# Loading the first x block as four tiles in turn on two DMA queues, with one warm-up matmul fewer

## The chip, the cores and the metric

The kernel runs on one core of a Trainium2 chip. The metric is the device time of one execution in microseconds, lower is better. The profile shows a span that is 1.2 to 1.3 us shorter than the device time of the same execution. The granted TensorE clock shown for whole runs is 1.0, except 0.994 in two runs (295.44 us in experiment 5, 295.73 us in experiment 8) and 0.999 in one of e11_split_evac. That number does not show the first microseconds, in which the clock is at half speed; these are read from the spacing of the matmuls and, where a trace has them, from its clock records.

"Landing" below means the moment at which the last of the 16 DMA engines reported its share of a transfer done, read from the completion records of the trace. The Trainium skill, "DMA: Bandwidth & Descriptors", section "Why a DMA increments its semaphore by 16 and not by 1", says that only the full 16 means that all data has landed.

## The reference, cut to what matters

```python
x = A_x                                              # [1, 2048, 640] bf16
g = sigmoid((x * gate_w).sum(-1, keepdims=True))
a = linear_attention(x, wqkv, w_phi) @ wo            # 32 heads of 20, phi = two softmaxes per head
b = (gelu(x @ w_gate) * (x @ w_up)) @ w_down         # F = 1728
out = g * a + (1 - g) * b
```

The change touches only the loading of the first 512 rows of x, for the v, k and q projections.

## The kernel before

Five engines run in parallel. Matmuls need x with its columns on partitions ("xT"). Tiles 0 to 3 (the first block) are loaded plainly, transposed on TensorE (PE) and copied out by VectorE (DVE) and ScalarE (ACT). Tiles 4 to 15 and the weights wk and wq are transposed by the DMA on the way in. Each DMA queue is served by one engine's sequencer, in order: "sp" and "act".

```python
def loads(self):
    x4 = self.x[0:self.BT, :].rearrange("(p j) n -> p j n", j=self.TB)    # 4 tiles, j = tile
    def xload(q, j):                                     # two tiles, 320 KB, one DMA
        sc.dma(q, lambda e: e.dma_start(self.xtok[:, j:j + 2, :], x4[:, j:j + 2, :]),
               writes=[("xtok", j), ("xtok", j + 1)])
    ...
    xload("sp", 0)
    xload("act", 2)
    sc.dma("act", ... w_phi ...)                         # 640 packets of 40 bytes
    for kt in range(KD):
        sc.dma("sp", ... w3[:, kt, 0:D] ...)             # "wv" blocks 0 to 4, 160 KB each
    sc.dma("act", ... gz ...)
    xturn(4, 2)                                          # transposed load, x tiles 4 and 5 (sp)
    wload(self.wkT, D, "wkT")                            # transposed load of wk (sp)
    xturn(6, 2)                                          # x tiles 6 and 7 (sp)
    wload(self.wqT, 0, "wqT")                            # transposed load of wq (sp)
    ...                                                  # further loads, all on sp

def attention_state(self):
    ...
    warm(7)                                              # matmuls on zeros
    xt(0, 6, "d"); xt(1, 7, "a"); xt(2, 2, "d"); xt(3, 3, "a")   # PE transposes and their copies
    for t in range(4): vs(t, 0)                          # V matmuls with wv block 0; then blocks 1 to 4
    ...
    self.v_early(4, 6); self.v_early(5, 0)
    f(0, "k", (2, 3), "d"); f(1, "k", (4, 5), "a")       # folds of wk; the letter: who copies, d = DVE
    self.v_early(6, 6)                                   # first use of x tile 6
    f(2, "k", (2, 3), "d"); f(3, "k", (4, 5), "a"); f(4, "k", (0, 1), "d")
    self.v_early(7, 6); self.k_early(0, 2)
    f(0, "q", (4, 5), "d"); f(1, "q", (6, 7), "d")       # first use of wqT
    self.k_early(1, 0)
    f(2, "q", (4, 5), "d"); f(3, "q", (6, 7), "d")
    self.k_early(2, 2)
    f(4, "q", (4, 5), "d")
    self.k_norm(0)                                       # DVE, 3.6 us for each tile from here on
    ...
```

A fold multiplies a block of wk or wq by w_phi on PE, so that the projection and the feature map become one product; its result is copied out by DVE or ACT. k_norm sums the exponentials of one k tile by head and divides by the sums.

The softmax here doesn't subtract the row's maximum and nothing guards it: scores larger than these inputs give would overflow.

## Time and profile before

| | before |
|---|---|
| device time, first three runs | 291.62, 291.98, 292.02 us |
| span, PE busy | 290.6 us, 282.1 us |
| x load on SP / on ACT landed | 4.79 / 4.55 us |
| first wv block landed | 5.45 us |
| x tiles 6 and 7 landed, wqT landed | 15.19 us, 20.29 us |
| DVE's first k_norm | 25.66 us |

From the page of the kernel before (first line, and the first line of its busy table: engine, busy us, share, instructions):

```profile
span 290.6 us, 6966 instructions
PE 282.1 (97%) x2990; PEld 179.2 (62%) x3007; DVE 167.5 (58%) x337; ACT 105.2 (36%) x199; POOL 27.6 (10%) x52
```

The PE is busy nearly throughout, so what remains is in single waits. The timeline of PE in the first 17 us (start us, length us, engine, line, operation, tiles, and in brackets the idle time before it):

```profile
1.25 3.17 PE L538 MATMUL ps<-zero 128*128 128x512 bf16 x7 [1.25 <-DVE zero L534]
4.83 1.29 PE L290 MATMUL ps<-ident,xtok 128*128 128x128 bf16 x20 [0.41 <-DMA xtok<-in_A_x_dram]
5.96 4.72 PE L363 MATMUL ps<-w,xT 128*128 128x480 bf16 x32
...
15.23 1.53 PE L351 MATMUL ps<-w,xT 128*128 128x512 bf16 x10
```

The seven warm-ups start 427 ns apart, the 20 transposes only 56 ns apart: 512 columns in 427 ns is about half the rate of 128 columns in 56 ns, so the full clock came in this trace just when the transposes began. The waits of PE in the first 52 us (who waited for whom: us in total, times, longest):

```profile
PE ps L538 <- DVE zero L534: 1.3, 1, 1.3
PE ps L449 <- DVE Ek L433: 1.2, 1, 1.2
PE ps L290 <- DMA xtok<-in_A_x_dram: 0.4, 1, 0.4
PE ps L351 <- ACT Eq L516: 0.3, 1, 0.3
```

The second line: at 50.9 us PE waits for the k_norm chain of DVE. The chain of waits, up to x tile 6 (start us, length us, what):

```profile
3.74 2.28 SPq L224
...
6.07 4.20 SPq L220
...
10.32 4.87 DMA xT<-in_A_x_dram
15.19 0.04 issue
```

Here the chain goes back through SP's issues of transposed loads (2.28 us for x tiles 4 and 5, 4.20 us for wk), not through PE. DVE, in its timeline, starts k_norm right behind the copy of the last fold of wq:

```profile
24.92 0.82 DVE L344 CAST wq<-ps 128x640 bf16<-128x640 f32 x1 [0.43 <-PE ps L331]
25.66 1.48 DVE L424 TENSOR_REDUCE Dk<-Ek 128x64 f32<-128x1280 bf16 x1
```

### The profile page before, as it was taken

To read this page: it belongs to the slowest core of one execution; us is meant where nothing else is said; L and a number is where in the kernel's file an instruction comes from. 1 tells how busy PE (TensorE), PEld (TensorE's weight loads), DVE (VectorE), ACT (ScalarE), POOL (GpSimd) and SP (SyncE) were. 2 spreads that over 40 slices of the span, in tenths; PEclk is the share of its full clock that TensorE was granted. 3 is DMA by queue.
4 is the path that set the end of the run, shared out by engine and by line. 5 is a ranking of instruction groups with operands and counts; after the bars stand their busy time and mean duration, and the time that the engine had idled before them with its cause. 6 is when DMAs were issued, how large, how long until landed. Compare 5 with 4: busy or idle time off the path is not lost.

```text
span 290.6 us, 6966 instructions
## 1 busy us (share of the span) xinstructions
PE 282.1 (97%) x2990; PEld 179.2 (62%) x3007; DVE 167.5 (58%) x337; ACT 105.2 (36%) x199; POOL 27.6 (10%) x52
## 2 busy tenths in 40 slices
PE   7999998999999999999999999999999999999996
PEld 3666788699954444444477644447764444777786
DVE  2248999999876742677767533235753323575001
ACT  3367887576673223222202232320223232022021
POOL 7000000000000000011131300001130000113000
PEclk9999999999999999999999999999999999999999
DMA  7999995000002000011114220000322000042211
GB/s 226 198 177 250 367 366 168 0 2 2 2 0 45 2 0 0 3 24 23 25 25 44 74 68 0 0 3 2 52 66 68 0 0 2 2 43 74 68 48 49
DMA packets 36937, 18.66 MB, mean 64 GB/s; under 512 B 28970, under 2 KB 36394, under 8 KB 36906
## 3 DMA queue, kind: packets, MB, share of 16 engines
q1 hardware_dynamic: 36096, 17.86, 25.9%
q8 instruction: 23, 0.38, 0.6%
q10 hardware_dynamic: 810, 0.35, 0.5%
q14 instruction: 8, 0.07, 0.1%
HBM read 9.04 MB, written 2.62 MB: 40 GB/s over the span
## 4 chain that ended last, share of the span: by engine, by line
PE 82%; DVE 8%; SPq 3%; issue 3%; DMA 2%; ACT 2%; ACTq 0%
PE ps L620 36%; PE ps L710 27%; PE ps L351 13%; DVE Dk L424 2%; PE ps L653 2%; DVE Ek L433 2%; DMA xT<-in_A_x_dram 2%; PE ps L630 1%; SPq L220 1%; DVE KV L504 1%; PE ps L449 1%; DVE Dk L428 1%; ACT Ek L413 1%; PE ps L331 1%; SPq L224 1%
## 5 line engine op out<-in xcount | busy, mean ns | idle before, releaser
L625 DVE TENSOR_TENSOR hT<-ps,gl 128x512 bf16<-128x512 f32 x52 | 35.8, 691 | 57.4 <-PE ps L620 56.6
L710 PE MATMUL ps<-wd_sb,hT 64*128 64x320 bf16 (+2 forms) x918 | 66.3, 288 | 0.0
L620 PE MATMUL ps<-xT,wu_sb 128*128 128x512 bf16 x256 | 63.8, 379 | 1.2 <-DVE hT L625 1.0
L620 PE MATMUL ps<-xT,wg_sb 128*128 128x512 bf16 x250 | 62.9, 379 | 1.3 <-issue 1.0
L623 ACT ACTIVATE gl<-ps 128x512 bf16<-128x512 f32 x52 | 31.0, 598 | 72.8 <-PE ps L620 66.3
L710 PEld LDWEIGHTS ps<-wd_sb,hT 64*128 64x128 bf16 x918 | 42.8, 94 | 15.4 <-ACT gl L623 0.8
L682 POOL TENSOR_TENSOR Og<-O,O 128x640 bf16<-128x640 bf16 x16 | 22.3, 1396 | 239.8 <-DVE O L680 239.8
L620 PEld LDWEIGHTS ps<-xT,wu_sb 128*128 128x128 bf16 x260 | 25.4, 98 | 32.0 <-DVE hT L625 1.5
L620 PEld LDWEIGHTS ps<-xT,wg_sb 128*128 128x128 bf16 x260 | 24.8, 98 | 30.1 <-issue 0.9
L723 ACT ACTIVATE outsb<-ps,Gm 128x320 bf16<-128x320 f32 (+2 forms) x31 | 14.6, 516 | 75.3 <-PE ps L710 75.3
L351 PE MATMUL ps<-w,xT 128*64 128x512 bf16 (+6 forms) x398 | 41.4, 325 | 0.2
L351 PEld LDWEIGHTS ps<-w,xT 128*64 128x64 bf16 (+1 forms) x400 | 33.4, 107 | 7.3 <-DMA xT<-in_A_x_dram 0.2
L710 PE MATMUL ps<-wo_sb,goT 64*128 64x320 bf16 (+2 forms) x340 | 27.3, 288 | 0.0
L351 PE MATMUL ps<-xT,wq 128*64 128x512 bf16 (+1 forms) x184 | 25.8, 380 | 0.4 <-ACT Eq L516 0.3
L433 DVE TENSOR_TENSOR Ek<-Ek,Dk 128x640 bf16<-128x640 bf16 x32 | 25.0, 822 | 0.6
L680 DVE TENSOR_TENSOR O<-ps,RH 128x640 bf16<-128x640 f32 x32 | 24.8, 817 | 0.0
L424 DVE TENSOR_REDUCE Dk<-Ek 128x64 f32<-128x1280 bf16 x16 | 23.7, 1481 | 1.5 <-ACT gcol L416 1.5
L516 ACT ACTIVATE Eq<-ps 128x512 bf16<-128x512 f32 x40 | 21.7, 605 | 2.6 <-PE ps L351 2.3
L413 ACT ACTIVATE Ek<-ps 128x640 bf16<-128x640 f32 x32 | 20.8, 704 | 3.5 <-PE ps L351 3.5
L710 PEld LDWEIGHTS ps<-wo_sb,goT 64*128 64x128 bf16 x340 | 16.2, 94 | 5.6
L351 PEld LDWEIGHTS ps<-xT,wq 128*64 128x64 bf16 (+1 forms) x185 | 14.5, 108 | 4.1 <-ACT Eq L516 0.8
L669 DVE RECIPROCAL RH<-ps 128x32 f32<-128x32 f32 x16 | 5.7, 358 | 17.3 <-PE ps L653 17.3
(65 smaller groups left out, 145.6 us busy)
## 6 DMA issues: line engine op xcount, KB each, us to landing
out_dram<-outsb SPq DMA_DIRECT2D x7, 320.0 KB, 2.5
wd_sb<-in_B_w_down_dram SPq DMA_DIRECT2D x1, 2080.0 KB, 13.9
wg_sb<-in_B_w_gate_dram SPq DMA_DIRECT2D x1, 1120.0 KB, 6.0
wu_sb<-in_B_w_up_dram SPq DMA_DIRECT2D x1, 1120.0 KB, 8.5
wg_sb<-in_B_w_gate_dram SPq DMA_DIRECT2D x1, 960.0 KB, 9.6
wu_sb<-in_B_w_up_dram SPq DMA_DIRECT2D x1, 960.0 KB, 10.2
w<-in_A_wqkv_dram SPq DMA_DIRECT2D x5, 160.0 KB, 4.2
wo_sb<-in_A_wo_dram SPq DMA_DIRECT2D x1, 800.0 KB, 9.6
```

Of the source, the lines that this page charges most:

```text
L351: self.sc.op("pe", lambda e: e.matmul(self.ps[a:z, bank * 512 + c0:bank * 512 + c0 + n], lhs[:, a:z], rhs, start=first, stop=fin), reads=r ...
L413: self.sc.op("act", lambda e, s=s, scale=scale: e.activation(self.Ek[:, se, s, :], self.ps[:, o:o + self.D], AF.Exp, scale=scale), reads=[ ...
L424: sc.op("dve", lambda e: e.tensor_reduce(self.Dk[:, se, 0, :].rearrange("p (s h) -> p s h", h=H), self.Ek[:, se, :, :].rearrange("p s (h d ...
L433: sc.op("dve", lambda e, v=v, r=r: e.tensor_tensor(v, v, r, ALU.mult), reads=[("Rk", se)], writes=[("Ek", se, s)])
L516: sc.op("act", lambda e, s=s, scale=scale: e.activation(self.Eq[:, s, i, b * self.BT:(b + 1) * self.BT], self.bank(bank), AF.Exp, scale=sc ...
L620: sc.op("pe", lambda e, kt=kt, w=w, bk=bk: e.matmul(self.bank(bk), w[:, kt, c * P:(c + 1) * P], xs(kt), start=(kt == 0), stop=(kt == self. ...
L623: sc.op("act", lambda e: e.activation(self.gl[:, slot, :], self.bank(banks[0]), AF.Gelu_apprx_tanh), reads=[("ps", banks[0])], writes=[("g ...
L625: sc.op("dve", lambda e: e.tensor_tensor(hT[:, c, :], self.bank(banks[1]), self.gl[:, slot, :], ALU.mult), reads=[("ps", banks[1]), ("gl", ...
L680: dve(lambda e, o=o, f=f, s=s: e.tensor_tensor(o, V[s][:, :, :, 0:DH], f, ALU.mult), rb + [key(6 + s)], [("O", s, sl)], guard=old)
L682: sc.op("pool", lambda e: e.tensor_tensor(self.Og[:, sl, :], self.O1[:, sl, :], self.O2[:, sl, :], ALU.add), reads=[("O", 0, sl), ("O", 1, ...
L710: sc.op("pe", lambda e: e.matmul(self.bank(bk, w), lhs, rhs, start=opens and x == 0, stop=end and not opens, skip_group_check=True), reads ...
L723: sc.op("act", lambda e: e.activation(dst, self.bank(bk, w), AF.Copy, scale=g), reads=rd, writes=wr)
```

## The change

The intent: tiles 0 and 1 land first, so the transposes start earlier, and one warm-up matmul gives them room. Each queue now issues two x loads of 160 KB in place of one of 320 KB. One packet carries 1280 bytes where it carried 2560.

```diff
         def xload(q, j):
-            sc.dma(q, lambda e: e.dma_start(self.xtok[:, j:j + 2, :], x4[:, j:j + 2, :]),
-                   writes=[("xtok", j), ("xtok", j + 1)])
+            sc.dma(q, lambda e: e.dma_start(self.xtok[:, j, :], x4[:, j, :]), writes=[("xtok", j)])
...
-        xload("sp", 0)
-        xload("act", 2)
+        for j in range(4):
+            xload(("sp", "act")[j % 2], j)
...
-        warm(7)
+        warm(6)
```

## The prediction

> **What bounds the kernel.** The page shows the PE busy 282.1 of 290.6 us: the whole is TensorE-bound. The change touches only the first 25 us. From the timeline and the DMA landings:
> - Seven warm-up matmuls run from 1.25 to about 4.3 us, 427 ns apart (half clock). The two 320 KB x loads (2560 B packets, 102 ns each) are issued at 0.80 on SP and ACT and land at 4.79 and 4.55. The PE waits 0.41 us for them (waits view); the 20 transposes start at 4.83, 56 ns apart (full clock).
> - The V matmuls start at 5.96 (first wv block landed 5.45). They wait twice (0.13 and 0.05 us) for ACT's xT copies of 0.70 us, then run without a gap to 11.8.
> - At 15.23 the PE waits about 0.22 us for the transposed load of x tiles 6 and 7, landed 15.19. The transposed wq load lands at 20.29, its first user runs at 20.34: almost no slack.
> - From 25.66 to 51 DVE runs k_norm without a pause, started by the last q fold; the PE waits 1.35 us for that chain at 50.9.
> - The chain of waits goes back from 15.19 not through the PE but through SP's issues.
>
> **What the change does.** Each queue issues two 160 KB x loads in place of one of 320 KB.
> - At 55 ns per 1280 B packet (as the wv blocks show) I estimate tiles 0 and 1 landed at 3.9 to 4.1, tiles 2 and 3 at about 4.9. The transposes begin at about 4.0 instead of 4.83. ACT's first copy moves up by about 0.5 us, so the fourth tile's V matmul starts at about 6.5 instead of 6.95, and V ends about 0.4 us earlier.
> - One more SP issue (412 ns and a gap, about 0.47 us) stands before the wv blocks and all transposed loads. The wv blocks hardly move, since the DMA engines are full from 2.9 to 7 us. The transposed loads move later by between 0 (if full engines hold up their issue: equal ones took SP 2.28 and 1.41 us) and 0.47 us.
> - The warm-up matmul saves nothing itself: left in, it would hold up tile 0's transposes by up to 0.4 us.
>
> **What reaches the end.** The 0.4 us won in V is lost at 15.2 us, where the PE meets the load of tiles 6 and 7, no earlier than before. The end moves with that landing: 0 to +0.5 us, my middle +0.2.
>
> Predicted: 292.2 us, range 291.6 to 292.9; faster by over 2%: 0.01, within 2%: 0.98, slower by over 2%: 0.01.
>
> **What would show it.** Right: transposes begin near 4.0, the last V matmul ends near 11.4; the wait before the v projection of tile 6 grows from 0.2 to 0.6 us or more; tiles 6 and 7 land at 15.2 to 15.7; the DVE chain starts at 25.7 to 26.1. Wrong: that landing at 15.0 or earlier and DVE's chain earlier, a gain.
>
> **What could make it wrong.** The clock. The Trainium skill, "TensorE: Matmul & The Clock Gate", Part 1, says that about 3.4 us of sustained matmuls release the full clock, by a free-running window. The trace agrees in size: matmuls from 1.25, full clock from 4.85. Part 4 says that transposes don't count as busy in the same way, which no trace here tests. With six warm-ups the PE is busy only to about 3.8; if the release slips a window (to about 8.3), V runs at half clock meanwhile, and I estimate +1 to +1.5 us at the end: one chance in ten. The other: transposed loads that land earlier because the split x load speeds the engines up.

## The result, and the profile after

| | before | after |
|---|---|---|
| device time, median (lowest to highest) | 292.0 (291.62 to 292.67), 4 runs | 292.56 (292.22 to 292.89), 4 runs |
| x tiles landed (0, 1, 2, 3) | 4.79, 4.79, 4.55, 4.55 | 4.08, 3.87, 4.85, 4.61 |
| first wv block landed | 5.45 | 6.23 |
| x tiles 6 and 7 landed | 15.19 | 15.79 |
| DVE's first k_norm | 25.66 | 26.26 |
| span | 290.6 | 291.2 |

The ratio was 1.0017, with a 95% interval of 0.9995 to 1.0038: the same. Ratios here are the mean time of one kernel's fast runs over that of the other's of the same rounds, so not quite the ratio of the medians. From the page of the kernel after:

```profile
span 291.2 us, 6985 instructions
PE 284.0 (98%) x3006; PEld 180.0 (62%) x3006; DVE 167.3 (57%) x337; ACT 105.2 (36%) x199; POOL 27.6 (9%) x52
```

PE shows more busy time and more instructions because the trace of before lacks some matmul records, not because of the change. The timeline of PE after:

```profile
1.25 2.74 PE L537 MATMUL ps<-zero 128*128 128x512 bf16 x6 [1.25 <-DVE zero L533]
4.13 1.99 PE L289 MATMUL ps<-ident,xtok 128*128 128x128 bf16 x20
6.37 4.53 PE L362 MATMUL ps<-w,xT 128*128 128x480 bf16 x32 [0.25 <-DVE xT L297]
...
15.84 1.36 PE L350 MATMUL ps<-w,xT 128*128 128x512 bf16 x7 [0.46 <-DMA xT<-in_A_x_dram]
```

The transposes start 0.70 us earlier but take 1.99 us instead of 1.29, because the first 14 of them run 107 ns apart, at half clock; the full clock came at 5.64 us. The V matmuls (third line) start 0.41 us later than before. The profile names a DVE copy of xT as what they waited for, but the first V matmul reads only tile 0, whose copy was done at 5.37. What fits is the first wv block, landed at 6.23: in four traces with split loads where it landed after the transposes, the first V matmul starts 0.14 us behind it (6.23 and 6.37 here; 6.65 and 6.79, 6.19 and 6.33, 6.45 and 6.59 in later runs). The waits (three other lines left out) and the chain after:

```profile
PE ps L448 <- DVE Ek L432: 1.2, 1, 1.2
PE ps L350 <- DMA xT<-in_A_x_dram: 0.5, 1, 0.5
```

```profile
4.24 2.25 SPq L223
...
6.54 3.54 SPq L219
...
10.12 5.67 DMA xT<-in_A_x_dram
15.79 0.05 issue
```

The wait for the x tiles (L350) is new. SP began its transposed loads 0.50 us later than before (4.24 against 3.74), and tiles 6 and 7 landed 0.60 us later. From there all of DVE's work lies 0.60 us later:

```profile
25.52 0.82 DVE L343 CAST wq<-ps 128x640 bf16<-128x640 f32 x1 [0.44 <-PE ps L330]
26.26 1.48 DVE L423 TENSOR_REDUCE Dk<-Ek 128x64 f32<-128x1280 bf16 x1
```

So these two traces tell a neat story: one more issue on SP, a later landing, 0.6 us at the end. The experiments show that only part of it holds.

### The profile page after: what moved, and what is told of

Read it like the earlier page. It is cut to its first block, busy times and chain, and to the rows that moved or that the text cites. A ratio compares the mean times of both kernels' runs of the same rounds, so it can differ in the third digit from the quotient of the medians.

```text
span 291.2 us, 6985 instructions
## 1 busy us (share of the span) xinstructions
PE 284.0 (98%) x3006; PEld 180.0 (62%) x3006; DVE 167.3 (57%) x337; ACT 105.2 (36%) x199; POOL 27.6 (9%) x52
## 4 chain that ended last, share of the span: by engine, by line
PE 83%; DVE 8%; SPq 3%; issue 2%; DMA 2%; ACT 1%; ACTq 0%
PE ps L619 36%; PE ps L709 27%; PE ps L350 13%; DVE Dk L423 2%; PE ps L652 2%; DMA xT<-in_A_x_dram 2%; DVE Ek L432 2%; PE ps L629 1%; PE ps L448 1%; DVE KV L503 1%; SPq L219 1%; DVE Dk L427 1%; PE ps L330 1%; SPq L232 1%; SPq L223 1%
## 5 line engine op out<-in xcount | busy, mean ns | idle before, releaser
L619 PE MATMUL ps<-xT,wu_sb 128*128 128x512 bf16 x260 | 64.6, 379 | 1.0 <-DVE hT L624 1.0
L619 PE MATMUL ps<-xT,wg_sb 128*128 128x512 bf16 x260 | 64.7, 379 | 0.0
L350 PE MATMUL ps<-w,xT 128*64 128x512 bf16 (+6 forms) x400 | 41.9, 325 | 0.5 <-DMA xT<-in_A_x_dram 0.5
L350 PEld LDWEIGHTS ps<-w,xT 128*64 128x64 bf16 (+1 forms) x400 | 33.4, 107 | 7.7 <-DMA xT<-in_A_x_dram 0.6
L350 PE MATMUL ps<-xT,wq 128*64 128x512 bf16 (+1 forms) x185 | 26.1, 380 | 0.3 <-ACT Eq L515 0.3
L350 PEld LDWEIGHTS ps<-xT,wq 128*64 128x64 bf16 (+1 forms) x185 | 14.6, 109 | 4.0 <-ACT Eq L515 0.8
```

The lines of the kernel that those rows point to most:

```text
L350: self.sc.op("pe", lambda e: e.matmul(self.ps[a:z, bank * 512 + c0:bank * 512 + c0 + n], lhs[:, a:z], rhs, start=first, stop=fin), reads=r ...
L619: sc.op("pe", lambda e, kt=kt, w=w, bk=bk: e.matmul(self.bank(bk), w[:, kt, c * P:(c + 1) * P], xs(kt), start=(kt == 0), stop=(kt == self. ...
```

## The experiments

**The measure used for all of them.** In the traces with unaltered copies (12 of 14, from 290.64 to 294.50 us), the end of the span is DVE's first k_norm plus 264.95 to 265.00 us. And in all 14 that start is, within 0.01 us, the latest of three sums:

- V gate: the start of the 40th (last) V matmul plus 13.83 us
- x gate: the landing of x tiles 6 and 7 plus 10.47 us
- wq gate: the landing of wqT plus 5.36 us

The three constants were read off single traces, and the others agree with them; they were on record before the traces from e6_pad3 on existed. In the two runs with moved copies 1.26 us, read off these two, is to be taken off each sum. The table has the latest gate in bold; "full clock" is the time at which the matmul spacing changes or the trace's clock record begins, a range where neither tells it closer. The experiments from e6 on ran on other chips than those before them (7 for e1 to e4, 0 for e6 to e9, 8 from e10 on), so times are compared with those of before in the same round, while traces are compared across rounds. By the 2% rule every verdict below is "same"; "slower" means here only that the interval leaves out no change.

| trace | full clock | first wv block | 40th V | V gate | x gate | wq gate | first k_norm | span |
|---|---|---|---|---|---|---|---|---|
| before | 4.85 | 5.45 | 11.60 | 25.43 | **25.66** | 25.65 | 25.66 | 290.64 |
| e13_before (before again) | 6.9 to 7.2 | 5.35 | 12.51 | **26.34** | 25.64 | 25.16 | 26.34 | 291.32 |
| after | 5.64 | 6.23 | 11.80 | 25.63 | **26.26** | 26.01 | 26.26 | 291.24 |
| e1_repeat (after again) | 6.0 to 6.8 | 6.65 | 12.22 | **26.05** | 25.81 | 25.28 | 26.05 | 291.05 |
| e2_split_warm7 | 5.91 | 5.68 | 11.74 | 25.57 | 25.80 | **26.29** | 26.29 | 291.28 |
| e3_whole_warm6 | 6.7 to 7.0 | 5.22 | 12.31 | **26.14** | 24.59 | 24.78 | 26.14 | 291.12 |
| e4_split_act3 | 4.98 | 4.59 | 12.15 | **25.98** | 25.40 | 24.93 | 25.98 | 290.95 |
| e6_pad3 | 6.80 | 5.88 | 12.38 | 26.21 | **27.09** | 25.53 | 27.09 | 292.06 |
| e7_whole_relief | 6.30 | 5.44 | 12.11 | 25.94 | 25.65 | **26.57** | 26.58 | 291.54 |
| e8_split_relief | 4.69 | 6.19 | 12.08 | 25.91 | **26.23** | 26.07 | 26.22 | 291.18 |
| e9_split_relief_w0 | 4.56, lost 7.97, back 11.38 | 5.85 | 15.72 | **29.55** | 27.56 | 26.91 | 29.55 | 294.50 |
| e10_whole_evac | 6.68 | 5.24 | 12.34 | **24.91** | 23.58 | 23.46 | 24.91 | 289.98 |
| e11_split_evac | 5.33 | 6.45 | 12.03 | 24.60 | 25.03 | **25.21** | 25.22 | 290.46 |
| e12_pairs | by 5.5 | 6.12 | 12.26 | 26.09 | **26.25** | 25.60 | 26.25 | 291.24 |

**1. The changed kernel again (e1_repeat).** No edit.

> The changed kernel once more, unaltered, for a second trace and more times. Theory S (the end moves with the transposed load of x tiles 6 and 7, and one more issue on SP delays that landing): landing again at 15.5 to 15.8 us, DVE's first k_norm at 26.0 to 26.3, time 0.4 to 0.7 us over the kernel before. Rival P (the first changed trace was unlucky: one 1280 B packet took 993 ns, and the last of 16 engines' share of the first wv block landed 0.75 us behind the others): no such packet here, first wv block lands at about 5.5 instead of 6.23, V starts by 5.6, and the end is within 0.2 us of before.

Median 292.05 us in 6 runs, before 292.18 in 11 runs (291.35 to 292.62); ratio 1.0002 (0.9985 to 1.0020). The repeat shows no loss at all. DVE's start, 26.05, fell where theory S put it, but for another reason than S has: tiles 6 and 7 landed at 15.34 and were not waited for; the V gate was last. Rival P falls too: the first wv block landed even later (6.65), with 15 of 16 engines done at 6.23. So a fixed cost of 0.4 to 0.7 us over before, which S expected, did not show; the interval (about -0.4 to +0.6 us) leaves room for its lower half.

**2. Split load, seven warm-ups (e2_split_warm7).**

```diff
-        warm(6)
+        warm(7)
```

> The changed kernel with the seventh warm-up matmul put back. Theory S: the warm-up plays no part in the end, so time within 0.2 us of the changed kernel, landing of tiles 6 and 7 again 15.5 to 15.8; the first transpose starts about 0.15 us later than 4.13. Rival C (six warm-ups release the full clock too late: it came at 5.64 us against 4.85 before, 14 transposes ran at half clock): full clock at 4.7 to 5.0, transposes done by about 5.6 instead of 6.1, and the end 0.3 us or more earlier than the changed kernel.

Median 292.08, ratio 1.0000 (0.9983 to 1.0017). The time does not notice the seventh warm-up. The full clock came at 5.91, later than in the trace with six (5.64), so rival C falls. Tiles 6 and 7 landed at 15.33, and the wq gate was last this time.

**3. Whole loads, six warm-ups (e3_whole_warm6).**

```diff
-        warm(7)
+        warm(6)
```

> The kernel before with six warm-up matmuls instead of seven, nothing else. Theory S: SP's issues are untouched, so tiles 6 and 7 land at about 15.2 and the end is within 0.15 us of before, even if the first transposes run at half clock. Rival C: the full clock comes late (5.5 us or later), V ends later, and the end is 0.3 us or more later.

Median 292.08, ratio 1.0001 (0.9983 to 1.0018). All 20 transposes ran at half clock, and the V gate was the last. This looked like C's prediction until experiment 12 showed the same with seven warm-ups. The time is that of before.

**4. Tile 0 on SP, tiles 1 to 3 on ACT (e4_split_act3).**

```diff
-            xload(("sp", "act")[j % 2], j)
+            xload(("sp", "act", "act", "act")[j], j)
```

The ACT queue also got six lanes, so that it never waits for one.

> The split load with tile 0 on SP and tiles 1, 2, 3 on the ACT queue (with six lanes there), so that SP issues as many transfers as before. Theory S: SP's transposed loads are issued at the times of before, tiles 6 and 7 land at 15.0 to 15.3, and the end is within 0.2 us of before (0.4 to 0.6 us faster than the changed kernel). Rival D (the smaller 1280 B packets cost the DMA engines time, whoever issues them): landing stays at 15.6 or later and the end 0.4 us or more above before.

Median 292.37, ratio 1.0014 (0.9998 to 1.0030): no clear difference. The landing of tiles 6 and 7 (14.93) came back to where it was, as theory S says, and still nothing was won: tiles 2 and 3 landed at 5.71 and 6.22, the last transpose started at 6.50, and the V gate was the latest. Opening one gate brought up the next.

**5. Three tiny loads more on SP (e6_pad3).** (No run bears the name e5. The line that allocates the tile pad is left out.)

```diff
         xload("act", 2)
+        for k in range(3):
+            sc.dma("sp", lambda e: e.dma_start(self.pad[:, k, :], self.x[k * P:(k + 1) * P, 0:16]), writes=[("pad", k)])
```

> The kernel before with three tiny loads (128 rows of 32 bytes, into a tile nobody reads) put on the SP queue between the x load and the first wv block: three more SP issues of about 0.47 us, almost no bytes. Theory G (the start of DVE's k_norm chain is the latest of three gates, and the end is that start plus 264.98 us: the 40th V matmul plus 13.83 us, the landing of x tiles 6 and 7 plus 10.47, the landing of wqT plus 5.36; one SP issue ahead delays the landings by up to 0.47 each): landing of tiles 6 and 7 1.0 to 1.5 us later than the 15.19 of before, DVE start 26.6 to 27.2, time 0.9 to 1.5 us over before. Rival A (the engines are so full that SP's issue order in time does not matter): landing within 0.4 us of before and time within 0.3 us.

Median 293.33, ratio 1.0063 (1.0041 to 1.0086): clearly slower. Chain of waits of this run (L231 are the tiny loads, two further ones left out):

```profile
1.27 0.43 SPq L231
...
5.17 2.20 SPq L225
...
11.41 5.21 DMA xT<-in_A_x_dram
16.62 0.05 issue
```

SP began its transposed loads at 5.17 instead of 3.74, and tiles 6 and 7 landed at 16.62 instead of 15.19: 1.43 us in both, 0.48 for each issue. So a later issue on SP does pass to the landing, with almost no bytes moved. That it passed to the hundredth is chance: with SP's transposed loads begun at 3.74 or 3.75, tiles 6 and 7 landed as early as 14.12 (experiment 3) and 14.37 (experiment 9). The mean loss of 1.84 us (0.0063 of 292) is more than theory G's 0.9 to 1.5, but one run of 295.44 us raises it, which shows a granted clock of 0.994; the medians lie 1.33 apart (293.33 and 292.00). The profiled run took 293.3.

**6. wv blocks 2 to 4 moved to the ACT queue, whole loads (e7_whole_relief).** The ACT queue also got eight lanes, as in experiments 7 and 8.

```diff
+        for kt in range(KD):
+            sc.dma("sp" if kt < 2 else "act", lambda e: e.dma_start(self.w3[:, kt, 0:D], w3[:, kt, 2 * D:3 * D]),
+                   writes=[("wv", kt)])
         sc.dma("act", ... w_phi ...)
-        for kt in range(KD):
-            sc.dma("sp", lambda e: e.dma_start(self.w3[:, kt, 0:D], w3[:, kt, 2 * D:3 * D]), writes=[("wv", kt)])
```

> The kernel before (whole x loads, seven warm-ups) with wv blocks 2, 3 and 4 issued on the ACT queue instead of SP, ahead of the w_phi load there. Theory G: SP reaches its transposed loads 1.4 us sooner, tiles 6 and 7 land at 13.7 to 14.5 and wqT by 19.5, both gates open; only the V gate stays, V ends as before (40th V matmul at 11.6 to 12.2), DVE start 25.4 to 26.0; time 0 to 0.4 us less than before. Rival A: landings within 0.4 us of before, no gain.

Median 292.42, ratio 1.0023 (1.0006 to 1.0040): slightly slower, not the gain of 0 to 0.4 us that G expected. SP's timeline in this run (the second and third lines are tiles 4 and 5, and wk):

```profile
1.28 0.88 SPq L230 DMA_DIRECT2D w<-in_A_wqkv_dram  x2
2.20 1.85 SPq L224 DMA_TRANSPOSE xT<-in_A_x_dram  x1
4.09 6.33 SPq L220 DMA_TRANSPOSE wkT<-in_A_wqkv_dram  x1
10.46 1.39 SPq L224 DMA_TRANSPOSE xT<-in_A_x_dram  x1
```

SP reached its first transposed load 1.54 us sooner (2.20 against 3.74), and tiles 6 and 7 landed at 15.18, as before (15.19). The issue of wk's load took 6.33 us instead of 4.20. What theory G expected of the landing was wrong, and rival A was right here. An issue that comes later delays the landing (experiment 5), one that comes earlier does not hasten it: SP is then held up in the next issue. The windows view fits a DMA that is the limit itself, though it does not prove it: from 7 to 11 us the DMA engines' share is 1.33 in this run and 1.19 before (packets overlap, so shares pass 1). The Trainium skill, "DMA: Bandwidth & Descriptors", section "Issuing engines are not separate DMA queues", says that issuing from several engines saves only the sequencer's time. This run agrees: 1.54 us of SP's time saved, 0.01 us of landing gained.

**7. The same with split loads (e8_split_relief).** The edit of experiment 6 in the changed kernel.

> The changed kernel (four x tiles, six warm-ups) with wv blocks 2, 3 and 4 on the ACT queue, ahead of w_phi. Theory G: the landing gates open as in the run with whole loads (tiles 6 and 7 by 14.7), so the earlier x tiles can pay: first V matmul at 5.6 to 6.1, 40th at 11.2 to 11.8, DVE start 25.0 to 25.6, time 0.3 to 0.8 us less than before. Rival W (V's start hangs on the first wv block and on the late full clock, not on x): first V matmul at 6.1 or later, DVE start 25.9 or later, no gain.

Median 292.53, ratio 1.0022 (1.0003 to 1.0040): slightly slower. The transposes started at 3.97, the full clock came at 4.69, the last transpose started at 5.37; and the V matmuls started only at 6.33, behind the first wv block (6.19). Even with early tiles and an early clock nothing is gained, as rival W says: wv sets V's start. In this trace an earlier V would not have helped either, since tiles 6 and 7 landed at 15.76 and the x gate (26.23) was later than the V gate (25.91).

**8. The first wv block between tiles 0 and 2 (e9_split_relief_w0).** SP issues tile 0, wv 0, tile 2, wv 1; ACT issues tiles 1 and 3, then wv 2 to 4. The edit against the changed kernel, shortened (vload is the load of one wv block):

```diff
-        for j in range(4):
-            xload(("sp", "act")[j % 2], j)
+        xload("sp", 0); xload("act", 1)
+        vload("sp", 0)
+        xload("act", 3); xload("sp", 2)
+        vload("sp", 1)
+        for kt in (2, 3, 4): vload("act", kt)
```

> The same with the first wv block issued on SP between x tiles 0 and 2 (SP: tile 0, wv 0, tile 2, wv 1; ACT: tiles 1 and 3, wv 2 to 4). Theory G with V's start held by the first wv block: it lands at 4.8 to 5.2, first V matmul right after the transposes at 5.3 to 6.1, and time equal to or up to 0.3 us less than the run with the block after both tiles. If tile 2 is what lands late instead (5.3 or later), the transposes end late and the gain is gone.

Median 294.01, ratio 1.0063 (1.0030 to 1.0095), with single runs from 292.19 to 295.73. Tile 2 landed at 8.12, 15 of 16 engines having been done at 6.89. The timeline of PE:

```profile
3.87 1.04 PE L296 MATMUL ps<-ident,xtok 128*128 128x128 bf16 x10
8.16 1.25 PE L296 MATMUL ps<-ident,xtok 128*128 128x128 bf16 x10 [3.25 <-DMA xtok<-in_A_x_dram]
9.20 5.61 PE L369 MATMUL ps<-w,xT 128*128 128x480 bf16 x32
```

The wait for tile 2 also cost the clock: by the trace's records it was full from 4.56, half from 7.97 and full again from 11.38 us. The second ten transposes run 107 ns apart again, and the V matmuls of 480 columns start 400 ns apart until 11.34 us, 202 ns after that. A load order that puts one needed tile last can lose more than any order here could win.

**9 and 10. Two copies moved from DVE to ACT, loads untouched (e10_whole_evac in the kernel before, e11_split_evac in the changed one).**

```diff
-        f(1, "q", (6, 7), "d")
+        f(1, "q", (6, 7), "a")
...
-        f(4, "q", (4, 5), "d")
+        f(4, "q", (4, 5), "a")
```

> The kernel before, loads untouched; two of the five copies of the folded wq (the second and the fifth) move from DVE to ACT, so DVE can begin k_norm without them. Theory G (in all traces so far the end is the start of DVE's k_norm chain plus 264.98 us): the chain starts at 24.4 to 24.9 instead of 25.7, the PE's wait of 1.35 us at 50.9 shrinks by about as much, and time is 0.5 to 1.0 us less than before, since ACT's delayed copies hold the PE up by at most 0.5 us earlier. Rival R (the end is set by the PE's own work, the DVE chain only goes along): the chain starts earlier, but time stays within 0.2 us of before.

> The same two copies moved in the changed kernel. Theory G with the load's effect washed out by noise of the three gates: time 0.4 to 1.0 us less than before, within 0.4 us of the run with whole loads. If the split load had a real cost, this one would be 0.5 us or more above that run.

Medians 291.57 and 291.59, before 291.78 in 11 runs; ratios 0.9985 (0.9964 to 1.0006) and 0.9986 (0.9965 to 1.0008). DVE's timeline with whole loads:

```profile
23.43 1.56 DVE L344 CAST wq<-ps 128x640 bf16<-128x640 f32 x2 [1.17 <-PE ps L331]
24.91 1.48 DVE L424 TENSOR_REDUCE Dk<-Ek 128x64 f32<-128x1280 bf16 x1
```

The chain starts at 24.91 although V was late in this trace (26.17 by the V gate without the edit). The waits of PE in the first 52 us:

```profile
PE ps L538 <- DVE zero L534: 1.3, 1, 1.3
PE ps L351 <- ACT Eq L516: 0.5, 1, 0.5
PE ps L290 <- DMA xtok<-in_A_x_dram: 0.3, 1, 0.3
```

The wait of 1.2 us for DVE's Ek is gone, and the span of 289.98 us is the shortest of all traces. The mean gain is about 0.4 us in both kernels (0.0015 and 0.0014 of 292), a little less than the 0.5 to 1.0 expected, and both intervals just include no change, so I do not call either faster. The two agree with each other to 0.02 us in the median, whichever way x is loaded. By their spans they agree less: the means are 290.07 and 290.33 us, against 290.70 before. With whole loads the device time lies further above the span than in any other kernel (1.47 us on average, not 1.2 to 1.3); why is not shown.

**11. Small packets with an unchanged number of issues (e12_pairs).** Each queue loads two tiles in one DMA as before, but tiles that are not neighbours, so packets are of 1280 bytes. The lists of written tiles are changed to match.

```diff
-            sc.dma(q, lambda e: e.dma_start(self.xtok[:, j:j + 2, :], x4[:, j:j + 2, :]),
+            sc.dma(q, lambda e: e.dma_start(self.xtok[:, j:j + 3:2, :], x4[:, j:j + 3:2, :]),
...
-        xload("act", 2)
+        xload("act", 1)
```

> The kernel before with the same two x loads and seven warm-ups, but each load takes two tiles that are not neighbours (0 and 2 on SP, 1 and 3 on ACT), so that its packets are of 1280 B instead of 2560 B and the number of issues stays. Theory Z (the small packets are what makes the first wv block land late: 5.68 to 6.65 us in four split kernels, 5.22 to 5.45 in three whole ones): x lands at about 4.9, the first wv block at 5.7 or later, with its last engine 0.8 us or more behind the first. Rival I (the additional SP issue does it): first wv block at 5.2 to 5.5. The end: within 0.5 us of before under both.

Median 293.77, ratio 1.0056 (1.0036 to 1.0077): clearly slower, against both theories' 0.5 us. The x load on SP landed at 5.45 instead of 4.79. The waits of PE show it:

```profile
PE ps L290 <- DMA xtok<-in_A_x_dram: 1.2, 1, 1.2
```

The first wv block landed at 6.12, as Z says (5.7 or later), but only because everything lay later: it came 0.67 us behind the x load, as with whole loads (0.66 and 0.63), and its engines finished within 0.68 us of each other, not 0.8 or more. So Z is not confirmed. Nor is the test clean: the number of issues stayed, but their time did not. SP's x load took 0.69 us to issue and the first wv block 0.82, against 0.41 and 0.42 before, so SP began its transposed loads at 4.30 instead of 3.74; tiles 6 and 7 landed at 15.78, and the x gate was last. The profiled run, at 292.52 us, was the fastest of the six (the others took 293.6 to 294.1), so the trace does not show what most of the loss was.

**12. The kernel before again (e13_before).** No edit, one look.

> The kernel before once more, for a second trace of it: the three gates vary by themselves. First wv block at 5.2 to 5.6, tiles 6 and 7 at 14.0 to 15.3, full clock anywhere from 4.7 to 6.7, DVE's chain from 25.5 to 26.2, end at that plus 264.98.

One run, 292.58 us. The timeline of PE, and the start of DVE's chain:

```profile
4.76 2.32 PE L290 MATMUL ps<-ident,xtok 128*128 128x128 bf16 x20 [0.34 <-DMA xtok<-in_A_x_dram]
6.87 4.73 PE L363 MATMUL ps<-w,xT 128*128 128x480 bf16 x32
```

```profile
26.34 1.48 DVE L424 TENSOR_REDUCE Dk<-Ek 128x64 f32<-128x1280 bf16 x1
```

This is the run that settles the neat story. The same program whose first trace ended at 290.64 ends here at 291.32, later than the first trace of the changed kernel (291.24). The loads landed as before (x at 4.72, first wv block at 5.35, tiles 6 and 7 at 15.17). The clock did not: all 20 transposes ran 107 ns apart, so they took 2.32 us instead of 1.29, and V's end moved by 0.91 us. Another chip is not needed to explain it: the 11 timed runs of before in this round, on the same chip as this one, lie between 291.22 and 293.0 us.

## Why the prediction was right

The predicted time of 292.2 us and its range held; the measured median was 292.56, and 292.05 in the repeat. That says little by itself: 28 of the 37 timed runs of before fall into the range of 291.6 to 292.9 too. And it rests in part on luck: the prediction has a gain in V that is lost at the x gate; the gain never came, and the sum is the same. Point by point:

- **What bounds the start: right.** The end goes with DVE's k_norm chain, and ahead of it stand V, tiles 6 and 7 and wqT with little between them. The prediction named all three. In the first trace of before they lay within 0.23 us (25.43, 25.66, 25.65).
- **Tiles earlier: right.** They landed at 3.87 and 4.08 (3.9 to 4.1 predicted), 4.61 and 4.85 (about 4.9); transposes began at 4.13 and 3.96 (about 4.0).
- **"The wv blocks hardly move": wrong, and this is the step that failed.** The first wv block landed at 6.23, 6.65 and 5.68 in the three traces with x split evenly over the queues and wv all on SP, and copies unaltered, against 5.22 to 5.45 in three with whole loads. "V ends about 0.4 us earlier" was wrong with it: the 40th V matmul started at 11.80 and 12.22 in the two traces of the changed kernel, against 11.60 and 12.51 before. Nothing was won in V that could have been lost at 15.2.
- **The x gate: right in mechanism.** With wv all on SP the landing of tiles 6 and 7 goes with SP's time. Where SP began its transposed loads at 3.63 to 3.75 they landed at 14.12 to 15.19 (five traces); at 4.23 to 4.30, at 15.33 to 15.82 (five, among them both of the changed kernel, 15.79 and 15.34, and experiment 11); at 5.17, at 16.62 (experiment 5). Of the changed kernel's two landings, 15.79 lies just above the predicted 15.2 to 15.7. The wait before tile 6 grew to 0.6 us in the first trace as predicted, counted as the prediction counts it (start to start, less the usual 0.06 us: 0.22 before, 0.62 after; the timeline, which counts from the modelled end, shows 0.46). In the repeat V was later still, and no wait was left.
- **The clock: the mechanism was real, its cause misjudged.** Six warm-ups were named as the risk. The full clock came anywhere between 4.6 and 7.2 us, with seven (4.85 to 7.2) as with six (4.56 to 7.0). V ran at half clock for more than its first matmul in no trace but that of experiment 8, where PE had waited 3.25 us. The size is what I missed: the late clock costs up to 1.0 us (20 transposes, 51 ns each), more than everything that the change does.

Where the gain went: the tiles' lead meets two things that the change does not touch or makes later, the clock and the first wv block; and then the two transposed loads. Pooled over both rounds the changed kernel's mean is 292.28 us in 10 runs and that of before 292.03 in 15; within a kernel the runs scatter by 1.3 us or more (before: 291.22 to 293.0 in 37 runs over all rounds). A true cost of 0.25 us cannot be told from none here.

**Open:** why the wv block lands late with split loads. In the changed kernel one packet of 1280 bytes took 993 ns where the median is 55, and the last of the 16 engines ended 0.75 us behind the others; but two kernels with whole loads have such packets of up to 801 and 904 ns (experiments 3 and 6), with the block at 5.22 and 5.44, experiment 11 shows small packets without such a straggler, and experiment 5 shows three more issues that cost this block 0.43 us (5.88 against 5.45). Nor is it shown which step made experiment 11 slow.

## What to carry to other kernels

Before believing a difference of half a microsecond between two traces, take a second trace of the same kernel: here two traces of one unaltered program differ by more than the change under test. Where several loads and a clock ramp arrive at one point within a few tenths of a microsecond, making one of them earlier wins nothing until all are; find that point and look at the work behind it, as the moved copies did. More issue time on a busy queue delayed what came behind it, but taking issues away won nothing here, where the next issue was held up instead.

## What the Trainium skill lacked or had wrong

- "TensorE: Matmul & The Clock Gate", Part 1, says that the window which releases the clock is free-running and varies by run, and this agrees: with the first matmul always at 1.25 us, the full clock came between 4.56 and about 7 us, and a wait of 3.25 us was enough to lose it. Its remark that the ramp costs less than 1% of a typical span holds too (an early or a late full clock differs by about 1.0 us of 291), but a change of 0.2% drowns in it; the page could say so.
- The same page, Part 4, says that the full clock does not engage for transposes. Here it does: in the first trace of before all 20 transposes start about 56 ns apart, the full rate, and in the changed kernel the clock was released at 5.64 us, when PE had run nothing but transposes since 4.13. (The kernel issues them as transposes; the trace lists them as MATMUL.) Whether a transpose counts as much as a matmul, no run tells.
- "DMA: Bandwidth & Descriptors" says that engines finish independently, but in the sections cited gives no size for it: here the last of the 16 ended 1.2 us behind the 15th in tile 2 of experiment 8 (8.12 and 6.89 us), and its consumer waited for the last.
- The section on issuing engines there says that several queues save only issue time. It lacks that the issue itself is held up: two transposed loads of the same size kept SP for 2.28 and 1.41 us in one trace, and the one of wk for 3.33 to 7.12 us over these kernels.
